# Moving single-input operations to GpSimd, turning C on TensorE, and laying spectra out by frequency tile in an S4 convolution kernel

## The chip, the cores and the metric

The kernel runs on one core of one Trainium2 chip. A core has TensorE (PE, matrix products into PSUM), VectorE (DVE), ScalarE (ACT), GpSimd (POOL) and SyncE (SP, which here only issues DMAs). The metric is the device time of one execution in microseconds, the median of several runs.

## The reference, cut to what matters

```python
x = A_u                                            # [1, 2048, 512] bf16
g = sigmoid((x * gate_w).sum(-1, keepdims=True))   # gate of every token
# A: S4 layer, 128 states per channel
dt = exp(log_dt)[:, None]
P  = exp((dt * (A_re + 1j*A_im))[:, :, None] * arange(L))
K  = einsum("dn,dnl,dn->dl", C_re + 1j*C_im, P, dt * (B_re + 1j*B_im)).real
a  = irfft(rfft(pad(x)) * rfft(pad(K)))[:L] + x * Dskip
# B: the two tokens with the largest x @ w_r go through a gated FFN
idx = argsort(-(x @ w_r))[:2]
xs  = x[idx]
y   = ((silu(xs @ w_gate) * (xs @ w_up)) @ w_down) * sigmoid(r[idx])
b   = x with y added to the rows idx
out = g * a + (1 - g) * b
```

Lags l are rounded to bf16 in the reference, so K takes few distinct values; the kernel computes it only at those lags.

## The kernel before

One block of code per engine is emitted from one list of operations (`P.add`, with the names below). Each operation has one or more alternatives, an engine and the planner's cost for it. `PLAN` is a written list of (operation, alternative) pairs: it fixes the engine of each operation and the order of each engine's queue; `BANKS` fixes the PSUM banks. Every engine works strictly in that order, waits on semaphores that follow from the buffers' overlaps (`emit_plan`), and a waiting instruction holds all behind it.

The channels are treated in two halves of 256 (c or hf = 0, 1), the tokens in two blocks of 1024 (m or j = 0, 1). The stages, with operation names:

1. **Parameters.** `nat0`..`nat3` load A_re, A_im, B_re, B_im by channel; `nt` turns them on TensorE (L512, a product with the identity). `cn4`, `cn5` load C_re and C_im by a transposing DMA (`DMAT`, L411). `al`, `bs`, `bn`, `bn2` make the decay and the phase per step; `w1`, `w2a`, `w2b`, `wr`, `wi`, `kwr`, `kwi` make the weights C*dt*B; `hi`, `lo` split the phase into two f16 parts.
2. **Angles and exponentials.** An angle is made either by TensorE (`pa`, L583 and L584, from `hi` and `lo`) or by a tensor_scalar from fp32 to int32 (`arg`, L564); ScalarE takes the sine of its low 16 bits (`sin`). `ep` (coarse lags) and `eq` (fine lags) are exponentials on ScalarE in pieces of 128x256. `ns` (L597) is a negated copy of a sine tile. `pi`, `pr` multiply the coarse table (region TP); `wpx`, `wpy`, `wpr`, `wpi` turn the weights by four phases, giving the fine weights WP from the phases PT; `px`, `py`, `s0`, `s1`, `qe` (function `unit`) make the fine table (region TQ), `qe464` being the last one of the second half of the channels.
3. **Forward transform of u.** `un` (L738) is -2 times the odd tokens of a block; `fw` (L723, and L727 for the corrections of block 1) are products with a cosine and sine matrix, `fwe` brings the spectra to region V (ScalarE L393 or VectorE L399). They are TensorE's filler between the other products.
4. **Kernel values and spectra, once per half.** `kmm` (L828) multiplies the coarse and the fine table, `kae` empties the PSUM, `sel` (L843) regroups, `kce` empties; `ks` (L860 to L865) gives the spectrum of K, `khe` empties it into KH.
5. **Products and inverse.** `prod`, `acc`, `yr`, `yi`, `pq` on VectorE multiply the spectra of u and K; `iv` (L934, L937) is the inverse transform, with the gated residual added by a product of the diagonal matrices RD (`rd`, L978) and U2; `ive` scales by g and stores; `out` writes. The last block (c=1, j=1) is done in two steps over the four frequency tiles of 128, as `KTS` says.
6. **Routing and FFN** in between: `log`, `gm` and the like find the two tokens, an indirect DMA of GpSimd (`gu`) gathers them, `ff` and `dn` are the FFN, an indirect DMA (`sc`) scatters the two rows into a copy of u in DRAM, from which U2 is loaded.

VectorE's tensor_tensor operations all have line L380, ScalarE's evictions L393, its other functions L402.

SBUF is cut into regions: U holds u (16 KB a partition), F the forward matrix, TP and TQ the tables, V the spectra of u, A the small fine tables, and later, each region holds other things as the dependencies allow. WP lies in U, over block 0 of u; PT lies in V. The spectra in V lie by block m, then odd or even part hc, then real or imaginary plane pl, then frequency tile kt.

Of the kernel before, what the change touches and what calls it, by code (L numbers as in the profile page):

```python
# [172 lines left out]
PLAN = [(0, 0), (4, 0), (5, 0), (7, 0), (3, 0), (1, 0), (23, 0), (6, 0), (26, 0), (227, 0), (2, 0), (11, 0), (8, 0), (12, 0), (242, 0), (9, 0), (14, 0),  # L173
(22, 0), (27, 0), (240, 0), (211, 0), (28, 0), (29, 0), (40, 0), (41, 0), (13, 0), (10, 0), (21, 0), (237, 0), (214, 0), (243, 0), (24, 0), (25, 0),
(134, 0), (226, 0), (228, 0), (257, 0), (223, 0), (109, 0), (215, 0), (137, 0), (212, 0), (135, 0), (110, 0), (224, 0), (112, 0), (136, 0), (31, 0),
(32, 0), (34, 0), (208, 0), (213, 0), (253, 0), (30, 0), (209, 0), (18, 0), (225, 0), (238, 0), (20, 0), (210, 0), (259, 0), (229, 0), (16, 0),
(207, 0), (111, 0), (36, 0), (216, 0), (33, 0), (230, 0), (138, 0), (114, 1), (19, 0), (217, 0), (35, 0), (113, 0), (218, 0), (141, 0), (144, 0),
(231, 0), (116, 0), (140, 0), (219, 0), (139, 0), (220, 0), (115, 0), (232, 0), (168, 0), (142, 0), (37, 0), (221, 0), (233, 0), (117, 0), (42, 0),
(169, 0), (120, 1), (234, 0), (118, 0), (43, 0), (45, 0), (244, 0), (145, 0), (88, 0), (170, 0), (278, 0), (274, 0), (222, 0), (46, 0), (119, 0),
(258, 0), (44, 0), (54, 0), (47, 0), (55, 0), (17, 0), (267, 0), (56, 0), (235, 0), (15, 0), (268, 0), (284, 0), (280, 0), (57, 0), (58, 0), (59, 0),  # L180
(124, 0), (75, 0), (236, 0), (125, 0), (282, 0), (273, 0), (60, 0), (121, 1), (61, 0), (279, 0), (252, 0), (254, 0), (38, 0), (62, 0), (281, 0),
(63, 0), (122, 0), (48, 0), (272, 0), (64, 0), (65, 0), (283, 0), (66, 0), (127, 1), (256, 0), (67, 0), (239, 0), (241, 0), (68, 0), (123, 0),
(286, 0), (69, 0), (76, 0), (70, 0), (271, 0), (255, 0), (82, 0), (71, 0), (171, 0), (39, 1), (72, 0), (146, 0), (143, 0), (73, 0), (160, 0),
(147, 0), (161, 0), (260, 0), (91, 0), (148, 0), (149, 0), (172, 0), (150, 0), (261, 0), (83, 0), (151, 0), (162, 0), (130, 0), (173, 0), (163, 0),
(152, 0), (153, 0), (262, 0), (126, 0), (263, 0), (245, 0), (84, 0), (49, 0), (154, 0), (174, 0), (131, 0), (128, 0), (129, 0), (246, 0), (247, 0),
(85, 0), (175, 0), (155, 0), (264, 0), (176, 0), (157, 0), (164, 0), (248, 0), (156, 0), (265, 0), (177, 0), (86, 0), (249, 0), (165, 0), (87, 0),
(158, 0), (378, 0), (250, 0), (166, 0), (133, 0), (132, 0), (266, 0), (89, 0), (251, 0), (167, 0), (363, 0), (379, 0), (77, 0), (90, 0), (100, 0),
(92, 0), (159, 0), (50, 0), (288, 0), (183, 0), (179, 0), (270, 0), (269, 0), (287, 0), (94, 0), (180, 0), (289, 0), (95, 0), (285, 0), (290, 0),
(276, 0), (178, 0), (364, 0), (184, 0), (291, 0), (93, 0), (181, 0), (292, 0), (380, 0), (294, 0), (96, 0), (365, 0), (185, 0), (293, 0), (97, 1),
(381, 0), (98, 0), (295, 0), (53, 0), (99, 0), (296, 0), (101, 0), (366, 0), (105, 0), (78, 0), (297, 0), (300, 0), (298, 0), (186, 0), (275, 0),  # L190
(187, 0), (51, 0), (299, 0), (389, 0), (277, 0), (301, 0), (182, 0), (362, 0), (360, 0), (376, 0), (302, 0), (303, 0), (188, 0), (382, 0), (189, 0),
(304, 0), (404, 0), (375, 0), (371, 0), (370, 0), (390, 0), (191, 0), (79, 0), (377, 0), (359, 0), (355, 0), (102, 0), (52, 0), (305, 0), (306, 0),
(107, 0), (192, 0), (307, 0), (358, 0), (403, 0), (372, 0), (80, 0), (308, 0), (194, 0), (367, 0), (309, 0), (361, 0), (190, 0), (312, 0), (408, 0),
(310, 0), (357, 0), (356, 0), (386, 0), (374, 0), (195, 0), (368, 0), (373, 0), (383, 0), (196, 0), (402, 0), (311, 0), (388, 0), (369, 0), (387, 0),
(393, 0), (193, 0), (385, 0), (384, 0), (401, 0), (199, 0), (197, 0), (313, 0), (391, 0), (314, 0), (392, 0), (201, 0), (436, 0), (394, 0), (315, 0),
(409, 0), (81, 0), (316, 0), (395, 0), (396, 0), (410, 0), (411, 0), (103, 0), (435, 0), (198, 0), (108, 0), (397, 0), (437, 0), (398, 0), (202, 0),
(406, 0), (412, 0), (407, 0), (326, 0), (399, 0), (405, 0), (327, 0), (400, 0), (328, 0), (200, 0), (413, 0), (329, 0), (330, 0), (414, 0), (203, 0),
(331, 0), (318, 0), (438, 0), (332, 0), (415, 0), (418, 0), (104, 0), (417, 0), (335, 0), (442, 0), (204, 0), (416, 0), (439, 0), (420, 0), (422, 0),
(440, 0), (333, 0), (317, 0), (336, 0), (334, 0), (441, 0), (106, 0), (319, 0), (427, 0), (443, 0), (419, 0), (421, 0), (444, 0), (425, 0), (424, 0),
(445, 0), (446, 0), (448, 0), (320, 0), (321, 0), (322, 0), (323, 0), (325, 0), (324, 0), (447, 0), (426, 0), (337, 0), (449, 0), (430, 0), (423, 0),  # L200
(450, 0), (428, 0), (429, 0), (451, 0), (454, 0), (338, 0), (452, 0), (453, 0), (206, 0), (455, 0), (205, 0), (456, 0), (345, 0), (457, 0), (431, 0),
(343, 0), (460, 0), (458, 0), (344, 0), (341, 0), (346, 0), (459, 0), (432, 0), (461, 0), (433, 0), (462, 0), (434, 0), (339, 0), (342, 0), (488, 0),
(351, 0), (340, 0), (463, 0), (349, 0), (352, 0), (487, 0), (347, 0), (350, 0), (353, 0), (348, 0), (464, 0), (354, 0), (489, 0), (465, 0), (466, 0),
(467, 0), (468, 0), (504, 0), (471, 0), (469, 0), (472, 0), (470, 0), (473, 0), (490, 0), (474, 0), (480, 0), (475, 0), (477, 0), (478, 0), (505, 0),
(476, 0), (484, 0), (485, 0), (481, 0), (479, 0), (492, 0), (482, 0), (491, 0), (483, 0), (503, 0), (531, 0), (502, 0), (486, 1), (525, 0), (527, 0),
(507, 0), (521, 0), (528, 0), (523, 0), (522, 0), (506, 0), (508, 0), (526, 0), (533, 0), (524, 0), (535, 0), (534, 0), (536, 0), (509, 0), (511, 0),
(510, 0), (529, 0), (494, 0), (538, 0), (532, 0), (537, 0), (539, 0), (530, 0), (493, 0), (496, 0), (554, 0), (495, 0), (500, 0), (499, 0), (497, 0),
(498, 0), (540, 0), (501, 0), (513, 0), (555, 0), (514, 0), (517, 0), (541, 0), (512, 0), (542, 0), (518, 0), (553, 0), (515, 0), (552, 0), (543, 0),
(519, 0), (557, 0), (544, 0), (556, 0), (545, 0), (558, 0), (547, 0), (559, 0), (546, 0), (549, 0), (561, 0), (560, 0), (575, 0), (550, 0), (548, 0),
# [839 lines left out]
```

## Time and profile before

| | |
|---|---|
| median of three runs | 177.0 us (176.63 to 177.24) |
| the profiled execution | 177.51 us, its span 175.7 us, granted clock 0.99 |
| TensorE busy | 152.3 us (87%), 1425 products |
| VectorE busy | 151.3 us (86%), 227 instructions |
| ScalarE busy | 128.6 us (73%) |
| GpSimd busy | 4.7 us (3%) |
| share of the chain that ended last | TensorE 79%, ScalarE 10%, DMA 5%, VectorE 2% |

The span is the time from the first to the last instruction of the program; the profiled execution's own time is 1.8 us more. A line of a group gives line, engine, operation, output and input with shapes, count, then busy us and mean ns of one, then the idle time of the engine ahead of them and who ended it. A line of a stretch gives start:end, its length, then busy us and count of PE, PE's weight loads, DVE, ACT and POOL, then the granted clock, the DMA share and GB/s.

### The profile page before, as it was taken

Reading aid. Unit: us, or ns where it says so; the run is one execution under the profiler, and the core shown is the slowest. Engines: PE = TensorE matmul, PEld = TensorE weight load, DVE = VectorE, ACT = ScalarE, POOL = GpSimd, SP = SyncE. Lnnn points to the kernel's source line nnn. Section 1 sums busy time; section 2 is a strip of 40 time slices with the busy share of each in tenths; the row PEclk is TensorE's granted clock in tenths of the full one; section 3 lists DMA queues with packets and bytes.
Section 4 is the critical chain, followed back from the end, with each engine's and each line's share of the span. In section 5 each row is a group of like instructions: output and inputs, shape, how many; then the busy total and the mean of one; then the engine's idle time right before and its main releaser. Section 6 shows DMA issues by size and latency. Waiting matters only on the chain.

```text
span 175.7 us, 3431 instructions
## 1 busy us (share of the span) xinstructions
PE 152.3 (87%) x1425; PEld 104.7 (60%) x1433; DVE 151.3 (86%) x227; ACT 128.6 (73%) x231; POOL 4.7 (3%) x10
## 2 busy tenths in 40 slices
PE   2339999999999999999996569989669999999992
PEld 1125656345568434445554448867358888888881
DVE  0755798999979899979898999799999999999932
ACT  4798089997989997998988776885587953711703
POOL 6000000000200000000002000000000000000000
PEclk9999999999999999999999969999999999999999
DMA  5999999975004950000042840000699000300084
GB/s 110 283 278 267 290 226 399 385 242 214 0 0 139 521 239 4 0 0 0 0 123 53 362 187 2 4 2 4 198 367 391 3 0 4 112 7 0 4 239 119
DMA packets 24211, 25.37 MB, mean 144 GB/s; under 512 B 12126, under 2 KB 20452, under 8 KB 23908
## 3 DMA queue, kind: packets, MB, share of 16 engines
q1 hardware_dynamic: 23538, 25.02, 44.9%
q8 instruction: 11, 0.18, 0.4%
q10 hardware_dynamic: 530, 0.13, 0.3%
q0 software_dynamic: 128, 0.01, 0.3%
q14 instruction: 4, 0.03, 0.1%
HBM read 20.70 MB, written 4.20 MB: 142 GB/s over the span
## 4 chain that ended last, share of the span: by engine, by line
PE 79%; ACT 10%; DMA 5%; DVE 2%; SPq 1%; issue 1%; ACTq 0%
PE psm L723 23%; PE psm L937 16%; PE psm L860 8%; ACT RB L393 7%; PE psm L828 6%; PE psm L583 6%; PE psm L584 5%; DMA RB<-in_A_B_im_dram 5%; PE psm L843 3%; PE psm L727 3%; ACT RB L402 2%; PE psm L934 2%; PE psm L693 2%; DVE RB L380 2%; PE psm L864 1%
## 5 line engine op out<-in xcount | busy, mean ns | idle before, releaser
L380 DVE TENSOR_TENSOR RB<-RB 128x1024 bf16<-128x1024 bf16 (+8 forms) x146 | 126.9, 907 | 5.4 <-ACT RB L393 2.0
L393 ACT ACTIVATE RB<-psm 128x1024 bf16<-128x1024 f32 (+4 forms) x43 | 40.1, 984 | 13.9 <-PE psm L828 5.0
L723 PE MATMUL psm<-RB 128*128 128x512 bf16 x184 | 45.2, 381 | 0.8
L402 ACT ACTIVATE RB<-RB 128x256 bf16<-128x256 f32 (+2 forms) x111 | 41.5, 453 | 2.4 <-DVE RB L380 1.9
L937 PE MATMUL psm<-RB 128*128 128x256 bf16 x256 | 31.5, 273 | 0.0
L723 PEld LDWEIGHTS psm<-RB 128*128 128x128 bf16 x192 | 17.9, 98 | 22.3 <-PE psm L727 1.7
L402 ACT ACTIVATE RB<-psm 128x1024 bf16<-128x1024 int16 (+1 forms) x23 | 22.4, 1009 | 7.3 <-PE psm L584 7.1
L937 PEld LDWEIGHTS psm<-RB 128*128 128x128 bf16 x256 | 25.1, 98 | 2.9
L948 ACT ACTIVATE RB<-psm,RB 128x256 bf16<-128x256 f32 x28 | 11.2, 478 | 19.0 <-PE psm L937 19.0
L584 PE MATMUL psm<-RB 128*128 128x256 f16 (+1 forms) x76 | 17.6, 297 | 0.0
L860 PE MATMUL psm<-RB 128*128 128x256 bf16 x128 | 15.8, 273 | 1.3 <-ACT RB L393 1.3
L583 PE MATMUL psm<-RB 128*128 128x256 f16 (+1 forms) x76 | 15.7, 305 | 0.7 <-ACT RB L402 0.3
L828 PE MATMUL psm<-RB 128*128 128x80 bf16 x256 | 12.3, 199 | 3.0 <-ACT RB L393 1.7
L860 PEld LDWEIGHTS psm<-RB 128*128 128x128 bf16 x128 | 12.4, 98 | 3.1 <-ACT RB L393 1.6
L828 PEld LDWEIGHTS psm<-RB 128*128 128x128 bf16 x256 | 10.1, 97 | 6.1 <-PE psm L828 2.5
L402 ACT ACT_TABLE_LOAD x9 | 11.5, 1283 | 1.9 <-PEq L1034 1.7
L583 PEld LDWEIGHTS psm<-RB 128*128 128x128 f16 x76 | 7.6, 103 | 3.8 <-ACT RB L402 0.8
L584 PEld LDWEIGHTS psm<-RB 128*128 128x128 f16 x76 | 7.4, 101 | 3.4 <-ACT RB L402 0.6
L934 PE MATMUL psm<-RB 128*128 128x256 bf16 x32 | 8.7, 273 | 0.0
L843 PE MATMUL psm<-RB 128*32 128x128 bf16 (+1 forms) x96 | 5.4, 391 | 3.6 <-ACT RB L393 3.6
L512 PE MATMUL psm<-RB 128*128 128x128 bf16 x16 | 2.4, 305 | 7.1 <-DMA RB<-in_A_B_im_dram 4.6
L864 PE MATMUL psm<-RB 128*128 128x256 bf16 x32 | 7.2, 273 | 1.3 <-ACT RB L393 1.3
(57 smaller groups left out, 95.8 us busy)
## 6 DMA issues: line engine op xcount, KB each, us to landing
RB<-in_A_u_dram SPq DMA_DIRECT2D x2, 1024.0 KB, 10.3
RB<-c_fwd SPq DMA_DIRECT2D x2, 1024.0 KB, 8.5
RB<-c_near SPq DMA_DIRECT2D x1, 2048.0 KB, 7.7
RB<-c_inv SPq DMA_DIRECT2D x1, 2048.0 KB, 7.8
RB<-u_routed SPq DMA_DIRECT2D x1, 2048.0 KB, 12.9
RB<-in_B_w_gate_dram SPq DMA_DIRECT2D x1, 1792.0 KB, 11.3
RB<-in_B_w_up_dram SPq DMA_DIRECT2D x1, 1792.0 KB, 7.0
RB<-in_B_w_down_dram SPq DMA_DIRECT2D x1, 1792.0 KB, 7.7
```

Source lines behind the costliest of these rows:

```text
L380: return P.add(name, [(DVE, c_dve(n, mode), lambda h: h.tensor_tensor(out=o(), in0=a_(), in1=b_(), op=op))], rd, wr, **kw)
L393: return lambda h: h.activation(out=o(), in_=a_(), func=ACTF.Copy, scale=scale() if callable(scale) else scale)
L402: return P.add(name, [(ACT, cost or c_act(n), lambda h: h.activation(out=o(), in_=a_(), func=func, scale=scale))], rd, wr, table=table, **kw)
L583: h.matmul(o, DGM(0, 128, (DPE.index(d) + 2) * 128, (1, 128)), HL(0, 128, k * 512 + c0, (1, w)), start=(k == 0 and i * w % 512 == 0), stop ...
L584: r = h.matmul(o, DGM(0, 128, 0, (1, 128)), DGM(0, 128, 128 + 1 - cs, (0, w)), start=False, stop=(cs == 0), skip_group_check=True)
L723: r = h.matmul(o, FM(0, 128, (par * 4 + q) * 1024 + pl * 512 + kt * 128, (1, 128)), x, start=(par == 0 and q == 0), stop=(hc == 1 and q == ...
L828: x = h.matmul(P32(t, q // 6, 0, 128, (q % 6) * 80, (1, 80)), TPv(0, 128, ri * 16384 + c * 8192 + r * 128, (1, 128)), TQv(0, 128, c * 1024 ...
L843: x = h.matmul(P32(t, jp, 32 * g, 32, c4, (256, nj), (4, 64)), CI(0, 128, 384 + 32 * c4, (1, 32)), KA(0, 128, (8 * jp + g) * 4 + c4, (16, ...
L860: x = h.matmul(o, KN(0, 128, g * 2048 + col, (1, 128)), KC[c](0, 128, g * 256, (1, 256)), start=(g == 0), stop=(g == NG - 1 and pl == 1))
L934: h.matmul(o, RD(0, 128, tb * 128, (1, 128)), U2(0, 128, tb * D + c * CW, (1, 256)), start=(q2 == 0), stop=False, skip_group_check=True)
L937: x = h.matmul(o, G(0, 128, (pl * 4 + k0_ + kt) * 1024 + (par * 4 + q) * 128, (1, 128)), PQ[j](0, 128, 2048 * par + 512 * k0_ + (pl * nk + ...
L948: r = h.activation(out=OT[k](0, 128, (4 * qp + 2 * q2 + par) * 256, (1, 256)), in_=P32(t, 0, 0, 128, q2 * 256, (1, 256)), func=ACTF.Copy, ...
```

## The change

- **C on TensorE.** C_re and C_im are loaded plainly like the other parameters (`nat4`, `nat5`), turned by eight more products (`nt4`, `nt5`) into a PSUM tile, and copied to SBUF (`cce`); `w1`, `w2a`, `w2b` read that copy.
- **GpSimd alternatives** for `arg`, `ns`, `un` and `rd`. The new plan gives GpSimd 13 of the 16 `arg` (two others go to ScalarE, one stays on VectorE), 7 of 8 `ns`, both `un`, and `rd`, which was on ScalarE.
- **Fine weights in place of their phases.** WP moves from U to the place of PT: `wpr`, `wpi` of a phase overwrite it.
- **Spectra by frequency tile.** The spectra of u and of K are laid out by frequency tile first; those of block 1 lie half in U and half in V. Accesses of `fw`, `fwe`, `khe`, `prod`, `yr`, `yi`, `pq`, `iv` change their strides accordingly, with innermost runs of 256 or more elements as before. `un` lies in the slots of the last spectrum part.
- `KTS` splits the last block's frequency tiles 2 and 2 instead of 3 and 1. RD and one output buffer move from U to V. The second, unused `sel` is gone.
- The planner's costs change, and with them the whole `PLAN` and `BANKS`: the order in every queue is new. Of VectorE and ScalarE, beyond the above, five spectrum evictions instead of four, `z0`, one `kae` and four `ive` instead of two are on VectorE; some tiny copies are on ScalarE. SP's order begins nat3, nat2, c_id, nat4, nat1, both parts of c_diag around Dskip, nat5, half of c_fwd, block 0 of u, the transposing load of u.

The core of the diff:

```diff
-KTS = ((0, 3), (3, 4))
+KTS = ((0, 2), (2, 4))
...
-            return 0.155 + n * {1: 1.04e-3, 2: 0.52e-3, 4: 0.27e-3}[mode]
+            return 0.14 + n * {1: 1.04e-3, 2: 0.52e-3, 4: 0.27e-3}[mode]
...
-            return 0.19 + n * 0.83e-3
+            return 0.10 + n * 0.83e-3
...
-        for k, i in enumerate((2, 3)):
+        for k, i in enumerate((2, 3, 4, 5)):
             nat(i, 2400.0 - 10 * k)
-        for i in (4, 5):
-            DMAT("cn%d" % i, lambda i=i: NAT(0, 128, i * 512, (512, 1), (1, 512)), lambda i=i: prm[i][:, :], [bNAT[i]], 128, first=2370.0 - i)
...
-        tB = P.pst(2, "tb")
-        for i in range(2):
-            turned(2 + i, tB, i)
+        tB, tC = P.pst(2, "tb"), P.pst(2, "tc")
+        for i in range(4):
+            turned(2 + i, (tB, tC)[i // 2], i % 2)
+        CC = at("TP", 58880, 2048, BF); bCC = bf_("cc", "TP", 58880, 2048)
+        EV("cce", row(CC, 0, 1024), lambda: P32(tC, 0, 0, 128, 0, (1, 1024)), [tC], [bCC], 1024)
...
-        TT("w1", row(W1, 0, 1024), pq_(tB, 0, 1024), row(NAT, 2048, 1024), ALU.mult, [tB] + bNAT[4:], [bW1], 1024, 1)
+        TT("w1", row(W1, 0, 1024), pq_(tB, 0, 1024), row(CC, 0, 1024), ALU.mult, [tB, bCC], [bW1], 1024, 1)
...
+                                  (POOL, 0.8, lambda h, o=o, t=t, off_=off_: h.tensor_scalar(out=o(), in0=BN(0, 128, 0, (1, D)), scalar1=-t, scalar2=off_, op0=ALU.mult, op1=ALU.add))], [bBN], [bARG[ak]])
...
+                             (POOL, 1.2, lambda h: h.tensor_scalar(out=o_(), in0=a_(), scalar1=-1.0, scalar2=None, op0=ALU.mult))], [bTRGc[k]], [bTRGn[k]])
...
+                         (POOL, 2.1, lambda h: h.tensor_scalar(out=o(), in0=a(), scalar1=-2.0, scalar2=None, op0=ALU.mult))], bU[m], [bUN[m]], behind=behind)
...
+        VL = [[("V", 0), ("V", 4096), ("V", 8192), ("V", 12288)], [("U", 0), ("U", 4096), ("V", 24576), ("V", 28672)]]
+        def vslots(m, hc, pl):
+            return [("sb", base[r] + o + (hc * 2 + pl) * 1024, base[r] + o + (hc * 2 + pl + 1) * 1024) for r, o in VL[m]]
...
-        WP = at("U", 0, 8192, BF)
+        WP = at("V", 16384, 8192, BF)
...
-                    vin = lambda: V(0, 128, m * 8192 + k0_ * 512 + c * CW, (2048, 4), (512, nk), (1, CW))
-                    kk = lambda: KH[c](0, 128, i * 4096 + pl * 1024 + k0_ * 256, (2048, 2), (0, 2), (256, nk), (1, 256))
+                        vin = lambda: V(0, 128, vo[m][k0_] + c * CW, (512, 4 * nk), (1, CW))
+                    kk = lambda: KH[c](0, 128, i * 4096 + k0_ * 1024 + pl * 256, (512, 2 * nk), (0, 2), (1, 256))
...
-                     (ACT, 5.6, rd_act)], [bCIA, bSGF["rr"]], [bRD])
+                     (ACT, 4.0, rd_act),
+                     (POOL, 4.8, lambda h: h.tensor_tensor(out=RD(0, 128, 0, (128, 16), (1, 128)), in0=CI(0, 128, 0, (0, 16), (1, 128)), in1=SGF["rr"](0, 128, 0, (1, 16), (0, 128)), op=ALU.mult))], [bCIA, bSGF["rr"]], [bRD])
```

81 lines of the change are left out of this document (41 added, 40 removed), and 77 rows, old and new, of the table PLAN.

## The prediction

> **What bounds the kernel now.** I read the stretches of the span first, then the waits, then the chain inside the widest gap, then the groups. The stretches (start:end, length, then busy us of each engine):
> ```profile
> 0.00:14.50 14.50, 5.30 (x29) 3.32 (x30) 5.65 (x11) 10.32 (x26) 2.70 (x8) 1.00 0.97 216
> 14.50:55.00 40.50, 39.52 (x324) 22.46 (x325) 36.81 (x80) 33.88 (x49) 0.94 (x1) 1.00 0.69 216
> 55.00:88.00 33.00, 32.58 (x216) 16.51 (x219) 30.28 (x61) 31.00 (x57) 0.00 (x0) 1.00 0.32 119
> 88.00:105.00 17.00, 11.70 (x190) 7.64 (x188) 15.65 (x23) 13.25 (x29) 1.07 (x1) 0.90 0.53 187
> 105.00:117.00 12.00, 11.53 (x104) 10.09 (x104) 10.72 (x12) 9.77 (x15) 0.00 (x0) 1.00 0.01 3
> 117.00:140.60 23.60, 19.96 (x280) 16.49 (x281) 23.50 (x16) 16.85 (x30) 0.00 (x0) 1.00 0.49 179
> 140.60:172.40 31.80, 31.69 (x291) 28.16 (x288) 28.37 (x28) 12.77 (x30) 0.00 (x0) 1.00 0.18 51
> ```
> TensorE (first busy column) is full except ahead of 14.5 us, in 88 to 105 (5.3 us idle) and in 117 to 140.6 (3.6). VectorE (third) is nearly as full from 14.5 on, ScalarE (fourth) to 88, GpSimd (fifth) empty. So three engines share the bound. The waits that name the early holes:
> ```profile
> DVE RB L380 <- PE psm L512: 4.8, 1, 4.8
> PE psm L512 <- DMA RB<-in_A_B_im_dram: 4.6, 1, 4.6
> ACT RB L402 <- PE psm L584: 7.1, 8, 4.4
> DVE RB L380 <- DMA RB<-in_A_C_im_dram: 3.2, 1, 3.2
> ```
> and the chain through the lag products of the first half of the channels (start, us, what):
> ```profile
> 90.95 1.84 ACT RB L393 x2
> ...
> 99.16 1.84 ACT RB L393 x2
> 101.04 2.71 PE psm L843 x42
> 103.78 1.25 ACT RB L393
> 105.07 4.10 PE psm L860 x36
> ```
> There TensorE waits for ScalarE to empty PSUM (`kae`, `kce`). The groups with the prices (count, busy, mean ns, idle before):
> ```profile
> L380 DVE TENSOR_TENSOR RB<-RB 128x1024 bf16<-128x1024 bf16 x74 | 49.0, 686 | 1.7 <-ACT RB L402 1.0
> L564 DVE TENSOR_SCALAR RB<-RB 128x512 int32<-128x512 f32 x16 | 6.5, 419 | 0.0
> L399 DVE CAST RB<-psm 128x1024 bf16<-128x1024 f32 x4 | 4.9, 1222 | 1.5 <-PE psm L723 1.5
> L978 ACT ACTIVATE RB<-RB 128x128 bf16<-128x128 bf16 x16 | 4.8, 392 | 0.0
> L597 DVE TENSOR_SCALAR RB<-RB 128x1024 bf16<-128x1024 bf16 x8 | 3.4, 423 | 1.6 <-ACT RB L402 1.5
> L738 DVE TENSOR_SCALAR RB<-RB 128x2048 bf16<-128x2048 bf16 x2 | 1.4, 690 | 0.4 <-DMA RB<-in_A_u_dram 0.4
> L534 POOL MEMSET RB<- 128x512 bf16 x1 | 0.6, 568 | 0.0
> L475 POOL MEMSET RB<- 128x128 bf16 x1 | 0.2, 205 | 0.3 <-POOLq L1034 0.3
> ```
>
> **Work moved between engines.** VectorE loses 15 of 16 `arg` (13 to GpSimd, 2 to ScalarE), 7 of 8 `ns` and both `un`: 15 x 0.42 + 7 x 0.42 + 2 x 0.69 = 10.6 us, and 1.2 us of tiny copies and the unused `sel`. It gains `cce` (1.22, the L399 row), one more spectrum eviction (1.22), `z0` (0.67, the 1x512 eviction), one `kae` of 320 (0.5, between the rows of 128 and 1024) and two `ive` (2 x 0.69): 5.0. Net -6.8; since VectorE records overlap by some 0.08 us, counted from start to start it is about -4.5, which I take. ScalarE loses `rd` (16 x 0.31 from start to start = 4.9), an eviction, `z0`, that `kae` and two `ive` (3.5 together), gains two `arg` and the tiny copies (2.1): about -6. TensorE gains 8 turning products (two groups of 0.5). GpSimd gains 13 `arg`, 7 `ns`, 2 `un`, `rd`. No row has it computing from SBUF; the two memsets give 0.08 + 0.95 ns an element: 0.57, 1.05, 2.02, 2.02, together 20.8 us. The planner's own costs in the diff (0.8, 1.2, 2.1, 4.8) give 27.8. I take the planner's, since those for VectorE and ScalarE beside them are within some 10% of the rows.
>
> **Start.** The two transposing loads of C leave SP's queue (4.99 and 2.19 us of issue, against 0.51 for a plain load), and with them the 3.2 us wait. But the new SP order puts B, C, A_im, all of c_diag (768 KB) and the 1 MB of c_fwd ahead of the first half of u: 3.7 MB. At the page's 110 GB/s in the first 4.4 us and some 280 after, u lands near 16 us (9.95 before). A_im, now fifth instead of third on SP, lands some 1.3 us later, so the f16 phases are ready at 10.6 (9.23). On TensorE the first angle products (2.6 us at the slow early rate that the trace shows, 12 of them from 11.96 to 14.52; to 13.2), B's turns (to 14.3) and the second angle tile (1.4 at full rate, to 15.7) come before the first `fw`; then `pa217` behind the sine of that tile (0.95; to 17.1), `k0` behind `w1`, `wr`, `kwr` on VectorE (14.6 + 1.22 + 0.69 + 0.60 = 17.1; to 17.7) and `pa160` (1.2): 18.9, instead of 14.4. Work done by then is 8.0 us instead of 3.3, so TensorE's lag (start minus own work queued ahead) is 10.9, not 11.1: no gain, no loss. u at 16 is covered by that; landing after 18.9 it isn't.
>
> **Middle.** I follow lags, with the work ahead of a step in the new order priced by the rows.
> - ScalarE: lag 5.6 at its first `ep`, nine table loads as before (11.5 us), 3.3 us of waits (for the first two angle tiles, later for `pa395`): first `kae` at 65.5 + 20.4 = 85.9; before 65.8 + 25.1 = 90.95. GpSimd's `arg` and `ns` are ready 1 to 15 us ahead of the sines and products that read them, except `ns412` and `ns397` (on GpSimd 1.2 us behind their sines), which hold VectorE 2.6 us; a wait for `eq` swallows that. The gather and scatter on GpSimd's queue stand behind these; the scatter issues at 85 (93 before).
> - TensorE: five `fw` (7.9 us) instead of two stand among the `kmm` and cover the evictions. It loses 3.1 us waiting for banks of angle tiles. Last `kae` 97.6, `sel`, `kce` to 101.2, spectra from 101.3 (105.06).
> - VectorE: 63.4 us ahead of the last fine product (69.5 before), then it waits for the exponentials of the second half: lag 17.7, first product at 87.9 + 17.7 = 105.6 (110.74), when its spectrum has just been evicted (104.9). `qe464`, which releases the second `kmm`, ends at 109.1; TensorE comes there at 112.7 (117.14).
>
> **Rest.** From the second `kmm` to the first `iv` stays 23.4 us (products and evictions unchanged; `rd` leaves ScalarE, but TensorE had no gap in those spectra): 136.1. 31.5 us of `iv`: 167.6. VectorE needs 56.3 us for all products and ends at 161.9, before the last four `iv` (3.5 us, twice as long with the 2/2 split) start at 164.1; so the split costs nothing; with VectorE later than 164.1 each us counts. U2 and G, 13 us after the last `kmm`, are covered as now. Tail 3.4. The span is 171.0 instead of 175.7: -4.7. The profiled execution took 177.51 (1.8 around its span), 0.5 over the median; I predict 177.0 - 4.7 = **172.3**.
>
> Edits costed at nothing: the weights in place (same four instructions; `wpr` no longer waits for the `fw` that free U, which was 0.17 us); the new strides of spectra and products (runs of 256 bf16 stay whole, so a 4096 product stays at its 2.29; at the fp32 rate, 1024 in 1.22, it would be double, and nothing in the layout asks for that); spectra of the second half stored into U (waits for `sin181`, long done).
>
> **Two engines at one memory.** No row shows VectorE beside a computing GpSimd. If they don't disturb each other it costs 0, and nothing could make it a gain. If each GpSimd instruction stops VectorE for its whole length, 19.8 us of those after the first four `arg` (9 x 0.8 + 7 x 1.2 + 2 x 2.1) meet a VectorE that is 91% busy, mostly with two-input instructions: 85% of them, which I estimate from that and the evictions from PSUM, are 16.8 us, less 4 us that it spends waiting for exponentials anyway, and 4.8 of `rd`: 17.6 us of delay. By the memset row it is 16.5 x 0.85 - 4 + 2 = 12.0. I take 0, since VectorE's rows next to GpSimd's two indirect DMAs (44.5 and 93.0 us) keep their lengths, though those don't compute. The Trainium skill, "SBUF — State Buffer", section "Who interferes with whom", speaks against it: a VectorE instruction with two SBUF inputs contends with a GpSimd instruction that reads SBUF, and whichever starts first blocks the other to its end. By that rule the sum would be the one of the first rival below; no run here shows it yet.
>
> **Rivals.** (1) Exclusion: VectorE, 17.6 us late, ends its products at 179.5; + 3.5 + 3.4 is a span of 186.4, **187.7**; by the memset row 12.0 late, **182.1**. For it: VectorE has hardly any idle time for GpSimd to fall into; against it: no row of VectorE beside GpSimd is longer than its group's mean. It decides where VectorE ends its products later than 175.7 - 6.9 = 168.8, so from 6.9 us of delay on (10.9 with the hidden 4): half of what GpSimd does beside it. (2) u late: landing at 22 instead of 16 costs 3 us of TensorE at the start, which nothing after wins back, and with one more sine late (1 us) it is **176.4**; for it the DMA rate of 110 GB/s in the first slice, against it that TensorE has 18.9 us of other things. (3) ScalarE free of its waits: TensorE's own work of 147 us behind a lag of 14 ends at 161.4, span 164.8: **166.1**; against it the lag of 20.4 by table loads alone.
>
> **How the numbers follow.** Forecast 0.47 (its own range 169.5 to 175.5, by 3 us of waits either way), ScalarE free 0.08, exclusion 0.33, u late 0.12 (of which 0.02 faster, 0.04 same, 0.06 slower). Faster by over 0.3%, about what a measurement of this kernel tells from none (its three runs span 0.35%): 0.57; same 0.04; slower 0.39. The range leaves out most of the free case and the upper third of the exclusion, where GpSimd costs all that the planner says: 168 to 186.
>
> **What would show it.** Right: first spectra (the L860 line's successor) near 101, `kmm` gap in 88 to 105 nearly closed, no C wait, DVE's 1024 row still 686 ns. Wrong: that mean over 800 ns, GpSimd spans of several us, TensorE waiting for VectorE at the second `kmm` or in the `iv`; for rival 2 a wait for in_A_u or c_fwd behind 16 us.

## The result and the profile after

The changed kernel takes 192.55 us (median of four runs, 192.33 to 192.66) against 177.12 us for the kernel before beside it: 1.084 times as long (95% interval 1.080 to 1.089). The forecast was 172.3, the range 168 to 186. The profiled execution took 192.33 us with a span of 190.5.

The stretches of the span, cut as in the prediction (start:end, length, busy us and count of PE, PE's weight loads, DVE, ACT and POOL, granted clock, DMA share, GB/s):

```profile
0.00:14.50 14.50, 6.83 (x45) 4.71 (x46) 5.72 (x8) 8.58 (x18) 5.69 (x12) 1.00 0.84 248
14.50:55.00 40.50, 36.01 (x320) 18.13 (x318) 37.35 (x69) 33.46 (x56) 20.59 (x13) 0.91 0.85 208
55.00:88.00 33.00, 29.28 (x154) 15.57 (x153) 28.14 (x40) 25.48 (x55) 11.36 (x4) 0.91 0.15 51
88.00:105.00 17.00, 15.27 (x129) 8.72 (x127) 12.98 (x15) 10.98 (x15) 9.23 (x3) 1.00 0.17 62
105.00:117.00 12.00, 8.36 (x130) 5.14 (x128) 11.41 (x19) 10.21 (x24) 0.00 (x0) 1.00 0.69 263
117.00:140.60 23.60, 19.55 (x276) 16.09 (x268) 23.22 (x18) 15.10 (x17) 4.58 (x2) 0.98 0.21 74
140.60:172.40 31.80, 29.14 (x277) 25.55 (x270) 31.70 (x23) 12.98 (x19) 0.00 (x0) 0.96 0.28 113
```

TensorE was full from 14.5 to 88 us before; now it misses 4.5 and 3.7 us there, and the clock is 0.91 in both stretches. VectorE looks no less busy than before, although work was taken from it: part of its "busy" is now waiting inside instructions, as the windows further down show. GpSimd is busy for 20.6 us of the second stretch alone. The spectra of the first half begin at 118.6 us (105.1 before, 101.3 forecast), so 13.6 of the 14.8 us by which the span grew are lost before them. The waits that are new (us in total, times, longest):

```profile
DVE RB L381 <- POOL RB L600: 6.7, 3, 2.8
ACT RB L403 <- POOL RB L567: 6.2, 2, 4.2
PE psm L728 <- DVE RB L400: 3.7, 1, 3.7
PE psm L511 <- DMA RB<-in_A_C_im_dram: 2.9, 1, 2.9
PE psm L728 <- POOL RB L745: 2.8, 1, 2.8
```

VectorE waits for `ns` (L600), ScalarE for `arg` (L567), and TensorE for `un` (L745): all three customers of GpSimd. TensorE's 3.7 us for VectorE's eviction (L400) come from GpSimd too: they stand behind the long product beside the second `un` that is shown below. The wait of 2.9 us for C on TensorE stands where before TensorE waited 4.6 us for B. In the chain that ended last GpSimd has 13% where it had none; two of its places (start, us, what):

```profile
17.23 2.78 POOL RB L600
20.01 3.40 POOL RB L567 x2
23.41 5.49 POOL RB L745
28.90 1.49 POOL RB L567
...
122.33 7.35 DVE RB L381 x3
```

The first four lines are one queue: an `ns` holds two `arg`, an `un` holds the next. The last line is a product that stands beside `rd`. The groups with the prices (count, busy, mean ns of one, idle before), and behind them two rows of the kernel before:

```profile
L381 DVE TENSOR_TENSOR RB<-RB 128x2048 bf16<-128x2048 bf16 x40 | 52.6, 1345 | 7.1 <-POOL RB L600 6.7
L381 DVE TENSOR_TENSOR RB<-RB 128x1024 bf16<-128x1024 bf16 x76 | 52.6, 706 | 1.6 <-ACT RB L403 0.2
L381 DVE TENSOR_TENSOR RB<-RB 128x4096 bf16<-128x4096 bf16 x10 | 26.2, 2666 | 0.0
L600 POOL TENSOR_SCALAR RB<-RB 128x1024 bf16<-128x1024 bf16 x7 | 20.4, 2916 | 37.2 <-ACT RB L403 23.2 <-ACT RB L394 14.0
L567 POOL TENSOR_SCALAR RB<-RB 128x512 int32<-128x512 f32 x13 | 11.7, 916 | 9.8 <-DVE RB L381 7.6 <-ACT RB L403 2.0
L745 POOL TENSOR_SCALAR RB<-RB 128x2048 bf16<-128x2048 bf16 x2 | 11.3, 5663 | 0.0
L381 DVE TENSOR_TENSOR RB<-RB 128x512 bf16<-128x512 bf16 x8 | 7.4, 919 | 0.1
L990 POOL TENSOR_TENSOR RB<-RB 128x2048 bf16<-128x2048 bf16 x1 | 3.6, 3622 | 0.0
...
L380 DVE TENSOR_TENSOR RB<-RB 128x2048 bf16<-128x2048 bf16 x28 | 33.5, 1221 | 1.2 <-ACT RB L402 1.0
L380 DVE TENSOR_TENSOR RB<-RB 128x4096 bf16<-128x4096 bf16 x10 | 22.5, 2287 | 1.1 <-ACT RB L393 1.1
```

Two things are to be read here. `ns` and `un`, bf16 to bf16, take 2.9 and 5.7 us on GpSimd, against the 1.2 and 2.1 of the planner; `arg` takes 0.9 (0.62 where nothing stands beside it), `rd` 3.6. Together that is 47 us, where the forecast had 27.8. And VectorE's products have become longer on average, 1345 against 1221 ns for 2048 elements, 2666 against 2287 for 4096. A mean hides that it happens to a few. Three windows, each set around one long VectorE instruction:

```profile
23.70:27.46 3.76, 2.56 (x12) 0.98 (x10) 3.73 (x1) 3.76 (x4) 3.76 (x1) 1.00 1.37 208
68.66:73.32 4.66, 4.66 (x23) 2.14 (x22) 4.66 (x3) 4.66 (x17) 4.66 (x1) 1.00 0.00 0
122.93:129.08 6.15, 6.15 (x59) 5.51 (x57) 6.15 (x3) 4.32 (x5) 3.94 (x2) 1.00 0.01 3
```

In the first, one product of 512 elements takes 3.73 us (419 ns in the run below that computes nothing on GpSimd) while one GpSimd instruction, `un`, runs through. In the second a 2048 product takes 4.65 beside the other `un`; in the third a 4096 product takes 6.12 beside `rd`. The stretching differs by kind: the trace has VectorE's neighbour longer by 3.3 and 3.4 us beside the two `un`, by 3.8 beside `rd`, by 0.7 to 0.8 beside three of the seven `ns` and by 0.3 beside a fourth, and by 0.3 to 0.9 beside some of the `arg`.

### The profile page after: what moved, and what is told of

Same layout as the page of the kernel before. It is cut to its first block, busy times and chain, and to the rows that moved or that the text cites. A ratio compares the mean times of both kernels' runs of the same rounds, so it can differ in the third digit from the quotient of the medians.

```text
span 190.5 us, 3448 instructions
## 1 busy us (share of the span) xinstructions
PE 159.4 (84%) x1441; PEld 107.0 (56%) x1441; DVE 164.2 (86%) x203; ACT 122.1 (64%) x215; POOL 51.4 (27%) x33
## 4 chain that ended last, share of the span: by engine, by line
PE 42%; ACT 19%; DVE 16%; POOL 13%; issue 5%; DMA 3%; SPq 2%
PE psm L945 15%; DVE RB L381 15%; ACT RB L403 12%; POOL RB L600 6%; ACT RB L394 6%; PE psm L728 5%; PE psm L867 4%; PE psm L835 4%; PE psm L585 3%; POOL RB L567 3%; PE psm L586 3%; POOL RB L745 3%; DMA RB<-in_A_C_im_dram 3%; PE psm L942 2%; PE psm L681 1%
## 5 line engine op out<-in xcount | busy, mean ns | idle before, releaser
L381 DVE TENSOR_TENSOR RB<-RB 128x1024 bf16<-128x1024 bf16 (+6 forms) x146 | 142.5, 1010 | 9.0 <-POOL RB L600 6.7
L728 PE MATMUL psm<-RB 128*128 128x512 bf16 x192 | 49.5, 401 | 6.6 <-DVE RB L400 3.7
L394 ACT ACTIVATE RB<-psm 128x1024 bf16<-128x1024 f32 (+4 forms) x41 | 38.5, 983 | 17.2 <-PE psm L869 4.9
L728 PEld LDWEIGHTS psm<-RB 128*128 128x128 bf16 x192 | 18.9, 102 | 29.1 <-issue 7.0
L945 PE MATMUL psm<-RB 128*128 128x256 bf16 x256 | 31.5, 273 | 0.0
L600 POOL TENSOR_SCALAR RB<-RB 128x1024 bf16<-128x1024 bf16 x7 | 20.4, 2916 | 37.2 <-ACT RB L403 23.2
L945 PEld LDWEIGHTS psm<-RB 128*128 128x128 bf16 x256 | 25.0, 98 | 2.9
L586 PE MATMUL psm<-RB 128*128 128x256 f16 (+1 forms) x76 | 19.0, 309 | 2.9 <-ACT RB L403 2.9
L956 ACT ACTIVATE RB<-psm,RB 128x256 bf16<-128x256 f32 x24 | 9.3, 495 | 17.0 <-PE psm L945 17.0
L585 PE MATMUL psm<-RB 128*128 128x256 f16 (+1 forms) x76 | 17.4, 329 | 0.0
L867 PE MATMUL psm<-RB 128*128 128x256 bf16 x128 | 16.2, 275 | 1.3 <-ACT RB L394 1.3
L567 POOL TENSOR_SCALAR RB<-RB 128x512 int32<-128x512 f32 x13 | 11.7, 916 | 9.8 <-DVE RB L381 7.6
L867 PEld LDWEIGHTS psm<-RB 128*128 128x128 bf16 x128 | 12.5, 99 | 3.2 <-ACT RB L394 1.6
L835 PEld LDWEIGHTS psm<-RB 128*128 128x128 bf16 x256 | 10.2, 97 | 5.9 <-PE psm L835 2.3
L745 POOL TENSOR_SCALAR RB<-RB 128x2048 bf16<-128x2048 bf16 x2 | 11.3, 5663 | 0.0
L942 PE MATMUL psm<-RB 128*128 128x256 bf16 x32 | 8.7, 272 | 1.3 <-ACT RB L394 1.3
```

The source lines that it names most:

```text
L381: return P.add(name, [(DVE, c_dve(n, mode), lambda h: h.tensor_tensor(out=o(), in0=a_(), in1=b_(), op=op))], rd, wr, **kw)
L394: return lambda h: h.activation(out=o(), in_=a_(), func=ACTF.Copy, scale=scale() if callable(scale) else scale)
L567: (POOL, 0.8, lambda h, o=o, t=t, off_=off_: h.tensor_scalar(out=o(), in0=BN(0, 128, 0, (1, D)), scalar1=-t, scalar2=off_, op0=ALU.mult, o ...
L585: h.matmul(o, DGM(0, 128, (DPE.index(d) + 2) * 128, (1, 128)), HL(0, 128, k * 512 + c0, (1, w)), start=(k == 0 and i * w % 512 == 0), stop ...
L586: r = h.matmul(o, DGM(0, 128, 0, (1, 128)), DGM(0, 128, 128 + 1 - cs, (0, w)), start=False, stop=(cs == 0), skip_group_check=True)
L600: (POOL, 1.2, lambda h: h.tensor_scalar(out=o_(), in0=a_(), scalar1=-1.0, scalar2=None, op0=ALU.mult))], [bTRGc[k]], [bTRGn[k]])
```

## The experiments

The theory after the result: GpSimd's instructions cost the time, by holding VectorE and by coming late. The rival: the new order and the rest of the change cost it. All differences below are against the kernel before in the same comparison (177.1 to 178.0 us); the change itself stands at +15.4 us.

**Nothing computed on GpSimd, the new order kept (a_none).** In the plan the alternatives of GpSimd go back, `arg`, `ns`, `un` to VectorE and `rd` to ScalarE:

```diff
-(136, 2) ... (236, 2) ... (111, 2) ... (488, 2)
+(136, 0) ... (236, 0) ... (111, 0) ... (488, 1)
```

> The changed kernel with nothing computed on GpSimd: the 13 arg, 7 ns and 2 un go back to VectorE and rd to ScalarE, at the same places of the order. Theory GpSimd (its instructions are long and shut VectorE out): the 51.4 us of GpSimd work and VectorE's lengthened products go, VectorE gets 9.8 us of its own back, and with some 4 us of that hidden the time is 172 to 178 us. Rival order (the new queues, the late first half of u, ScalarE's waits are what costs, GpSimd only stands beside): 187 us or more.

185.42 us, +7.5 (ratio 1.041, 1.035 to 1.046): neither. **Only the 13 `arg` on GpSimd (a_args):**

```diff
-(236, 2) ... (111, 2) ... (488, 2)
+(236, 0) ... (111, 0) ... (488, 1)
```

> The changed kernel with only the 13 arg on GpSimd; ns and un back on VectorE, rd on ScalarE. Theory GpSimd: an arg takes 0.62 us there when nothing is beside it, 8 us in all, of which most meets VectorE work, against 13 x 0.42 = 5.5 us saved on VectorE: within 2 us of the kernel with nothing on GpSimd, 172 to 179. If the length of ns and un (2.8 and 5.5 us) weren't the matter but any GpSimd work, about half of the loss stays: 180 to 186. Rival order: 187 or more.

182.26 us, +4.4 (1.024, 1.019 to 1.030): 3 us less than with the `arg` on VectorE. The time falls where the expectation put "any GpSimd work", but not for that reason, as the next runs show. Part of the 3 us can be TensorE's clock: a granted clock of 0.963 over 184.7 us and of 0.980 over 180.2 us are 13.7 and 7.2 us at half clock. **The other way round: the kernel before, its order unchanged, with GpSimd's 13 `arg`, 7 `ns`, 2 `un` and `rd` (b_pool)**; the edit is the new alternatives of the diff and 23 entries of the old plan:

```diff
-(134, 0) ... (234, 0) ... (109, 0) ... (486, 1)
+(134, 2) ... (234, 2) ... (109, 2) ... (486, 2)
```

> The kernel before, its order and layouts, with only the 13 arg, 7 ns, both un and rd given to GpSimd. Theory GpSimd: VectorE saves 9.8 us of its own, but 13 x 0.65 + 7 x 2.8 + 2 x 5.5 + 3.6 = 42.7 us of GpSimd instructions shut it out or keep it waiting for a result: 185 to 197 us. Rival order: the moves alone make it no slower, 170 to 178 us.

192.43 us, +14.5 (1.083, 1.075 to 1.090). The moves alone, without any of the other edits, cost as much as the whole change. That leaves the +7.5 of the first run to be explained, and the chain of the run with the `arg` on GpSimd points at most of it (start, us, what):

```profile
120.57 1.83 ACT RB L389 x2
122.40 4.66 ACT RB L981 x16
127.06 2.89 ACT RB L389 x4
130.00 2.71 PE psm L845 x42
```

`rd` (L981), put back on ScalarE at the place that was written for GpSimd, stands among the evictions (L389) for which TensorE's `sel` (L845) waits. If so, it is a cost of my experiment, not of the order; the next run tests it.

**`rd` on ScalarE behind `kce` (a_args_rd), and `rd` on GpSimd at its place (a_args_rdp)**, both with the 13 `arg` on GpSimd and `ns`, `un` on VectorE:

```diff
-(488, 1), (491, 0) ... (485, 0), (504, 0)
+(491, 0) ... (485, 0), (488, 1), (504, 0)
```

> The kernel after with the 13 args on GpSimd, everything else of GpSimd on VectorE and ScalarE, and rd on ScalarE behind the kce of the second half instead of ahead of it. Theory (the 5.9 us hole of TensorE ahead of the second half's sel, 1.7 in before, is rd standing on ScalarE between kae and kce, a place that was chosen for a GpSimd rd): the hole goes back to 1.7 us and the kernel takes 182.3 - 4.2 = 178 us (177.5 to 179). Rival (the hole is the order of the kae themselves, or rd is missed by iv afterwards): over 181 us.

177.93 us, +0.4 (1.003, 1.000 to 1.006), as the theory had it: the place of `rd` was worth 4.0 us of the 7.5, and the 3 us of the `arg` are nearly all of the rest.

> The same as the kernel with only the args on GpSimd, and rd on GpSimd too. Theory of exclusion: ScalarE's hole of 4.2 us goes, but the 4096 product beside rd is stretched by some 3.8 us as in the kernel after; VectorE has no slack there, so 180.5 to 182.3 us, and by comparison with the run that puts rd behind kce, rd costs 3 to 4 us. Rival (VectorE has slack there, or ScalarE's rd was the dearer): 178 us or less.

180.06 us, +2.5 (1.014, 1.008 to 1.019). So `rd` on GpSimd costs 2.1 us against a well placed `rd` on ScalarE, less than the 3 to 4 expected. **The order before with only the 13 `arg` (b_args), and with only `ns` and `un` on GpSimd (b_ns):**

```diff
-(134, 0) ... (234, 0) ... (109, 0)
+(134, 2) ... (234, 0) ... (109, 0)     # b_args, 13 arg
+(134, 0) ... (234, 2) ... (109, 2)     # b_ns, 7 ns and 2 un
```

> The kernel before with only 13 args on GpSimd, order unchanged. Theory (an arg on GpSimd takes 0.62 us, stretches VectorE little, 2.6 us in all against the 5.5 us that VectorE saves): 175 to 177 us. Rival (TensorE and ScalarE set the end in that part, so VectorE's gain buys nothing): 177.5 to 178.5 us. If the args on GpSimd are late for the sines: over 179 us.

177.20 us, -0.3 (0.997, 0.994 to 1.000), between the two expectations. VectorE's busy time fell by 1.1 us only (151.3 to 150.2), not by 5.5.

> The kernel before with only 7 ns and the 2 un on GpSimd (bf16 to bf16), order unchanged. Theory (the bf16 instructions, 2.8 us and 5.6 us each, are what costs: late results and locked VectorE): 187 to 191 us, most of the 14.5 us of the run with all four kinds. Rival (rd, or all kinds alike by their busy time): 183 to 186 us.

187.68 us, +10.2 (1.054, 1.048 to 1.060). The `arg` cost nothing in either order, the bf16 `ns` and `un` most: 10.2 of the 14.5 us in the order before. The other 4 us of that run go with `rd`, or with all of them standing in one queue; no run there separates these. **`arg`, the two `un` and `rd` on GpSimd, `ns` on VectorE, in the new order (a_un):**

```diff
-(236, 2)
+(236, 0)     # and the six others
```

> The kernel after with ns on VectorE: args, the two un and rd on GpSimd. Against the run with args and rd on GpSimd (180.1 us). Theory (cost goes with GpSimd's busy time on bf16 reads: un is 11.3 us of 32): 183 to 185 us. Rival A (un is dearer, since its VectorE neighbours were stretched by 3.3 and 3.4 us and TensorE waits 2.8 us for it): 186 to 189 us. Rival B (un costs little, ns nearly all of the 12.5 us): 180 to 182 us.

185.20 us, +7.2 (1.039, 1.032 to 1.045), hardly above the theory's 183 to 185. From +0.4 the steps are therefore 2.1 for `rd`, 4.7 for two `un`, and 8.2 for seven `ns`, up to the +15.4 of the change.

**What holds whom: six GpSimd instructions put beside VectorE's products of the kernel before (b_probe).** They work on scratch that nothing else reads:

```diff
+for behind_, f in ((488, fill), (491, read16), (510, read32), (542, read16), (556, fill), (570, read16)):
+    P.add("probe", [(POOL, 1.0, f)], [] if f is fill else [bSCR], [bSCR]).deps.add(P.ops[behind_])
```

> The kernel before with six more GpSimd instructions on a scratch tile that nobody reads, each started behind one VectorE instruction of the product phase: a memset of 1024 bf16, a tensor_scalar of 1024 bf16, one of 512 fp32 to int32, again bf16, again the memset, and one bf16 behind the last product, where VectorE idles. Theory exclusion: beside the three reading ones a VectorE product lasts longer by about what the GpSimd instruction takes (2.8, 0.6, 2.8 us), beside the memsets it keeps its 2.29 or 1.22 us; the last one takes 2.8 us alone; VectorE ends its products 3 to 6 us later and the time rises by 1 to 4. Rival (GpSimd is only slow, and the long VectorE records were waits for data): all products keep their lengths, and the time stays at 177 within 1.

One run, 178.7 us, against 177.9 (177.1 to 178.9) for the kernel before: no difference that one run can tell. Four windows of it, around a memset, around a bf16 read while products follow each other without a gap, around its end, and around the end of an fp32 read:

```profile
114.27:115.30 1.03, 1.03 (x12) 0.92 (x10) 0.59 (x1) 0.94 (x2) 0.95 (x1) 1.00 0.06 16
127.36:136.07 8.71, 7.37 (x91) 5.95 (x84) 8.71 (x4) 6.82 (x18) 8.71 (x1) 0.84 0.96 373
136.08:138.72 2.64, 2.64 (x26) 2.37 (x25) 2.58 (x2) 1.48 (x3) 2.63 (x1) 1.00 0.55 206
143.81:146.52 2.71, 2.71 (x28) 2.42 (x26) 2.70 (x2) 0.36 (x1) 0.57 (x1) 1.00 0.00 0
```

The memset takes its 0.95 us and no neighbour is longer. The bf16 read starts at 127.36, and while VectorE goes through its four products of 4096 at 2.29 us each, GpSimd gets nothing done that the trace shows: it ends at 138.71, 11.35 us for 2.7 us of work. Only behind a break of 0.04 us in VectorE's row at 136.07 does it get in, and then a 2048 product takes 1.94 instead of 1.22. The second bf16 read went the same way: 9.22 us beside four products of 3072 that kept their 1.75, and 0.7 us for the product behind the next break. The fp32 read needed no break: it started at 141.78, took 2.60 us for 0.62 us of work, and got in between two overlapping 4096 products, the second of which is 2.70 us long (last window). So the two engines do hold each other up. Beside gapless products it was mostly GpSimd that paid, and VectorE lost 0.4 to 0.7 us each time.

The Trainium skill, "SBUF — State Buffer", section "Who interferes with whom", states that a two-input VectorE instruction contends with a GpSimd instruction that reads SBUF, not with one that only writes it, and that whoever issues first blocks the other fully, for the whole instruction. The first half agrees with this trace: VectorE's products are longer beside reads and keep their lengths beside memsets. The second half doesn't: while the bf16 read got its 2.63 us from 136.08 to 138.71 (third window), VectorE lost only 0.7 us, and in the changed kernel an `ns` of 2.76 us beside VectorE's gapless row at 65.4 us lengthened one 2048 product to 2.05 us and left the 1024 product behind it, still beside the `ns`, at 0.68. The `un`, with 3.4 of 5.8 us, and `rd`, with 3.8 of 3.6, come nearer to the rule. Why an `ns` holds VectorE for so much less than its length, no run here shows.

**Late without reading (a_late).** Each `ns` and `un` becomes three memsets of its tile, one behind the other: as long as before, the same instructions wait for them, but nothing is read.

```diff
-(POOL, 1.2, lambda h: h.tensor_scalar(out=o_(), in0=a_(), scalar1=-1.0, scalar2=None, op0=ALU.mult))
+(POOL, 1.2, lambda h: h.memset(o_(), 0.0))    # and two more ahead of it
```

> The kernel after, with each ns and un of GpSimd replaced by three memsets of the same tile (0.95 us for 1024, some 2.85 us a tile, against 2.77 of the ns; un some 5.7): GpSimd's results come as late as before, the same instructions wait for them, but GpSimd reads nothing from SBUF. The values of those tiles are left out (zeros), so is their effect on the output. Theory of exclusion: VectorE isn't stretched beside them, and of the 12.5 us that ns and un cost, most goes: 181 to 185 us. Rival (lateness of the results costs, not the shared memory): 189 to 192.5 us.

187.18 us (185.40 to 188.97), +9.2 (1.048, 1.041 to 1.054): between the two. The groups of VectorE and the waits, from the trace of the longest of its four runs:

```profile
L378 DVE TENSOR_TENSOR RB<-RB 128x1024 bf16<-128x1024 bf16 x76 | 51.9, 698 | 1.4
L378 DVE TENSOR_TENSOR RB<-RB 128x2048 bf16<-128x2048 bf16 x40 | 47.6, 1220 | 7.8 <-POOL RB L600 7.4
```

```profile
DVE RB L378 <- POOL RB L600: 7.4, 4, 3.0
ACT RB L400 <- POOL RB L564: 6.0, 2, 3.5
PE psm L728 <- POOL RB L748: 3.5, 2, 3.2
```

The 2048 products are back at 1220 ns, the waits for GpSimd are all still there. So both the shared memory and the lateness cost: of the 12.9 us of `ns` and `un` (15.4 - 2.5), some 6 go with the shared memory (15.4 - 9.2) and some 7 are lateness alone (9.2 - 2.5). The runs of this kernel spread over 3.6 us, and its GpSimd work is 1 us shorter (50.3 us busy against 51.4), so the split is good to an us or two. Each part holds what the clock of TensorE added behind the waits (last section).

**`ns`, `un` and `rd` at the price that the forecast's lower row gave them (a_memset):** one memset each, 0.95 and some 1.8 to 2.0 us, no reads.

> The kernel after with each ns, un and rd of GpSimd replaced by one memset of the same tile (0.95 us for 1024, 1.8 for 2048), the args left as they are: what those instructions should have cost by the memset rows, with nothing read from SBUF. Their values are left out (zeros). If all of the miss lies in what GpSimd's instructions cost, the order is worth what the forecast said: 171.5 to 174 us. If the order itself is worth less than forecast (work on TensorE and its half clock, VectorE as the next bound): 175 to 179 us.

177.11 us, -0.35 (0.998, 0.995 to 1.000). This is the order that the forecast priced at -4.7 us, with 22.0 us of moved work on GpSimd, between the forecast's two prices of 20.8 and 27.8, and with only 0.6 us of waits for GpSimd left, on VectorE. So GpSimd's bf16 work and `rd` explain 15.8 us of the miss, and another 4.3 lie in the forecast of the order. It also says what the moves are worth at best: with `ns`, `un` and a well placed `rd` on VectorE and ScalarE the same order took +0.4 us, so even at the price of a memset they buy 0.8. Its TensorE, the last lag products of the first half and the first spectra (start, us, idle before):

```profile
96.64 2.89 PE L835 MATMUL psm<-RB 128*128 128x80 bf16 x56
101.16 2.69 PE L850 MATMUL psm<-RB 128*32 128x128 bf16 x48 [1.64 <-ACT RB L394]
105.19 0.28 PE L871 MATMUL psm<-RB 128*128 128x256 bf16 x1 [1.34 <-ACT RB L394]
```

The spectra begin at 105.19, as before (105.07), not at 101.3. TensorE has no hole above 0.45 us from 33.6 to 99.5. Up to the end of these lag products it idles 10.2 us (12.7 before), as the front and the filler `fw` promised; but it is busy for 89.3 us (86.4 before). Of these 2.9 us, the two groups of C's turning products are 1.2 (0.58 each at the early rate), and a stretch of 3.4 us at half clock at 49.2 is up to 1.7; that sum is an account, no run took the two away.

**The half clock (a_ff, a_ff2b).** In the kernel with the `arg` on GpSimd (177.93) the clock is halved twice ahead of the first spectra. The stretch ahead of each and the stretch itself:

```profile
28.40:30.70 2.30, 1.74 (x64) 1.79 (x66) 2.30 (x4) 2.01 (x5) 1.95 (x3) 1.00 0.86 188
31.10:34.50 3.40, 3.40 (x9) 1.22 (x8) 2.11 (x7) 3.40 (x13) 0.00 (x0) 0.50 1.06 392
48.00:50.80 2.80, 2.80 (x113) 2.80 (x114) 2.80 (x5) 2.78 (x5) 0.00 (x0) 1.00 0.04 7
51.60:55.00 3.40, 3.18 (x13) 1.83 (x13) 3.26 (x7) 3.37 (x7) 0.00 (x0) 0.50 1.07 356
```

Ahead of each stand the 64 and 112 products of two columns of `log` and `ff`. I moved the second group of `ff` (94 in the plan) away from the first, behind an angle product, and then, together with its PSUM copy `ffe` (95), also behind a group of `fw`:

```diff
-(91, 0) ... (94, 0), (102, 0) ... (262, 0), (295, 0) ... (95, 0), (245, 0), (131, 0)
+(91, 0) ... (102, 0) ... (262, 0), (94, 0), (295, 0) ... (95, 0), (245, 0), (131, 0)     # a_ff
+(91, 0) ... (102, 0) ... (262, 0), (295, 0) ... (245, 0), (131, 0), (94, 0), (95, 0)     # a_ff2b
```

> The kernel with only the args on GpSimd and rd behind kce (177.9 us), with one change of order on TensorE: the second group of 56 FFN products of two columns comes one angle product (pa, 128x512) and some small work later, instead of straight behind the first group. Theory (a stretch of 3.4 us in which TensorE streams few columns, here 112 products of two columns in a row, is followed by 3.4 us at half clock, seen at 51.6 us): the half-clock stretch at 51.6 goes and the kernel takes 1 to 1.7 us less, 176.2 to 177. Rival (the clock falls there for another reason, or TensorE isn't the bound behind it): 177.5 to 178.3 and the stretch stays, or goes with no gain.

180.03 us, +2.0 (1.011, 1.007 to 1.014), and the half clock lasts 6.8 us.

> As the run that moved the second group of FFN products behind one angle product (180.0 us, where the half-clock stretch at 50.8 grew to 6.8 us), but with one more group of products of u (fw, eight of 512 columns, 1.7 us) between the two groups, so that no stretch of 3.4 us holds mostly two-column products; the PSUM copy of the second group (ffe) moves with it. Theory (few columns streamed in a window halve the clock in the next): no half-clock stretch near 51, 176 to 177 us against 177.9 of the kernel with the groups back to back. Rival (splitting itself is what cost 2 us, by the later FFN or by the waits of the angle product, and the clock follows from that): 179 us or more.

180.40 us, +2.7 (1.013, 1.009 to 1.017). The stretch is still there, and VectorE, which comes to the copy (`ffe`) of the second group before the products are done, waits:

```profile
DVE RB L392 <- PE psm L676: 3.9, 1, 3.9
```

The first run is over both expectations, the second as its rival had it: splitting the FFN cost 1.6 and 2.3 us against the +0.4 of the unsplit kernel, in the second run by this wait as far as its trace shows. The theory of the two-column products is neither borne out nor refuted by it: in the 3.4 us ahead of the stretch at 50.2 TensorE still had the 56 products of the first group and 0.8 us without work. What sets the half clock in these places stays open.

**A version for use (b_kae).** The kernel before with the `arg` on GpSimd, and the last but one `kae` of the first half on VectorE:

```diff
-(323, 0), (325, 0), (324, 0)
+(323, 0), (325, 1), (324, 0)
```

> The kernel before with only the 13 args on GpSimd (177.2 us) and one PSUM eviction of the first half (the kae of 480 columns ahead of the last one) on VectorE instead of ScalarE, so that the last two run side by side. Theory (TensorE waits 1.9 us for ScalarE's last two kae ahead of sel, and VectorE has some 2 us in hand since the args are gone): 0.5 to 1.5 us less, 175.7 to 176.7. Rival (VectorE's fine products are then late for the second kmm by as much): 177 to 178.

176.98 us, -0.6 (0.996, 0.992 to 0.999): the only run with its whole interval under the kernel before, by half a per cent. It doesn't differ measurably from the 177.20 with the `arg` alone, and TensorE waits about as long as there ahead of that `sel`, now for VectorE's own eviction (1.9 us for ScalarE's with the `arg` alone):

```profile
PE psm L842 <- DVE RB L395: 1.8, 1, 1.8
```

VectorE comes out of a row of products and starts it 0.5 us behind ScalarE's; its 1.15 us end 0.6 us after ScalarE's 0.97.

## Why the prediction was wrong, point by point

- **Work moved between engines.** The term that was mis-sized is GpSimd: 27.8 us by the planner's costs, 47 measured. The planner's costs were taken because those of VectorE and ScalarE beside them agreed with the rows; that says nothing of a third engine that had no row. It holds for `arg` (0.8 against 0.9), fails for bf16 inputs by 2.4 and 2.7 times, and was too high for `rd` (4.8 against 3.6). VectorE's net of -4.5 us had the right sign but was too large: with nothing on GpSimd it is busy for 156.6 us; the 22 moved instructions are 9.8 of that by the rows of before, 8.0 with the prediction's overlap of 0.08 us taken off each, which leaves 148.6 against 151.3, so -2.7. ScalarE's -6 was right (128.6 to 122.1 in the run with memsets).
- **Start.** The first `fw` at 18.75 us (18.9 forecast), no wait for u or c_fwd, TensorE's idle time ahead of it no longer than before: right. That C's wait would be gone was wrong: TensorE waits 2.9 us for its load, and VectorE, which waited 3.2 us for C, now waits 2.2 us for the turned tiles in its place.
- **Middle, GpSimd 1 to 15 us ahead.** Wrong: the 6.7, 6.2 and 2.8 us of waits above. An `ns` and an `un` ahead of the `arg` in the same queue are 3.3 us at the planner's costs; in the chain above they are 8.3, so 5 us of the slack were not there. Lateness alone is some 7 us.
- **Middle, TensorE.** Wrong by 4 us even with cheap GpSimd work: first `kae` at 88.97 instead of 85.9, spectra at 105.19 instead of 101.3. The step followed ScalarE's lag to the first `kae` and took the five `fw` as cover. TensorE's holes did shrink by 2.5 us, but it had 2.9 us more busy time in that part and hardly a hole from 33.6 us on, so what VectorE and ScalarE gained bought nothing. It was nearly full there before the change too (1.4 us idle from 14.5 to 88 us), as the prediction's first paragraph had read.
- **Rest.** Right as a difference: from first spectra to first `iv` 34.9 us in the run with memsets (34.8 forecast; 37.1 in the changed kernel, where VectorE stands beside `rd`), 31.6 us of `iv`, the 2/2 split and the layout free (a 4096 product stays at 2287 ns).
- **Two engines at one memory.** The value 0 was wrong, and so was the reason for it: that rows beside indirect DMAs kept their length is no evidence on instructions that compute. By the group means VectorE lost 40 x (1345 - 1221) + 76 x (706 - 686) + 10 x (2666 - 2287) + 8 x (919 - 419) ns = 14.3 us; some 6 us of the time went with that for `ns` and `un`, and `rd` cost 2.1 by itself. The Trainium skill, "SBUF — State Buffer", section "Who interferes with whom", which the prediction set against its own choice, was right that the two contend; blocking for the whole length, as the rival had it too, was too hard on the `ns`.
- **The rivals.** The first (187.7) had the direction and half of the mechanism, and came within 5 us by luck: it had 27.8 us of GpSimd time for 47, no lateness, and a cost only from VectorE's end; the loss came in the first half of the channels, in all three queues. Its sign, a 1024 row over 800 ns, did not show (706): the stretching fell on a few instructions. The other two did not occur.

## What to carry to other kernels

An engine that has no row in the trace has no price: run its cheapest and dearest instruction beside the real neighbours once before a planner's cost is believed. Work moved to a slow engine in a strict queue is late by all that is queued ahead of it, and VectorE with two-input products and GpSimd with reads hold each other up, so their times can't be summed as if they were independent. When three engines are all near full, taking work from two of them is worth nothing until the third has been summed as well.

## What the runs showed of the hardware that I had not expected

- GpSimd on one input: 512 elements fp32 to int32 take 0.62 us with nothing beside them, 1024 elements bf16 to bf16 2.77 with VectorE idle (62.68 us in the changed kernel): 1.2 against 2.7 ns an element. The two `un` of 2048 bf16 elements took 2.7 and 2.8 ns an element. Which of the differences between `arg` and the others makes this, the types or the operation, was not separated. A memset of 1024 takes 0.95.
- Which of the two engines is held isn't settled by the recorded starts: beside the probe VectorE's gapless products held GpSimd for 8.7 us, while `rd`, recorded 0.35 us later than a 4096 product, took the 3.62 us that it takes in three other runs and the product took 6.12.
- Besides those at the very end, every half-clock stretch lasts 3.4 or 6.8 us, and ahead of the last lag products of the first half the changed kernel has 13.7 us of them, the kernel before none. Over the whole span a granted clock of 0.955 over 190.5 us and of 0.990 over 175.7 us are 17.1 and 3.5 us at half clock, so up to 6.8 of the 15.4 us can be the clock. Three windows of the changed kernel, cut just inside such stretches:

```profile
30.50:37.30 6.80, 6.57 (x59) 2.84 (x57) 4.54 (x10) 5.41 (x11) 4.70 (x6) 0.50 1.05 403
54.40:57.80 3.40, 3.40 (x15) 1.80 (x13) 3.26 (x7) 3.36 (x8) 0.00 (x0) 0.50 1.03 357
78.30:81.70 3.40, 3.40 (x15) 1.98 (x14) 3.37 (x6) 0.00 (x0) 0.00 (x0) 0.50 0.02 5
```

The first and the last follow waits of TensorE for GpSimd and VectorE of 2.8 and 3.7 us, so a late result may be paid again in the clock, by up to half of such a stretch; no run tested that by itself. The Trainium skill, "TensorE: Matmul & The Clock Gate", Part 1, gives a free-running window of 3413 ns, which agrees with these lengths (3.41 and 6.83 us); it has the clock fall after an idle window, while here it also falls behind a stretch in which TensorE's records leave no gap, though most of its products have two columns (48.0 to 50.8 us above).
